# Attention loop regrouped into periods of two head pairs, in an attention and expert-layer kernel

## The chip, the cores and the metric

The kernel runs on one core of a Trainium2 chip. The metric is device time in microseconds (us) for one whole execution: attention over all heads, the routing of tokens to experts, and the expert layers. Five engines work side by side, each through its own queue of instructions in the order of the program: TensorE (PE, with its weight loads PEld), VectorE (DVE), ScalarE (ACT), GpSimd (POOL) and SyncE (SP). An instruction that waits for another engine holds up everything behind it in its own queue.

## The reference: what is computed

```python
def _attn_ref(q, k, v):                      # 8 batches, 12 heads, 448 positions, 64 per head
    scores = scale * np.matmul(q, k.transpose(0, 1, 3, 2)) - np.log(S)
    attn = 1.0 / (1.0 + np.exp(-scores))     # sigmoid, no softmax
    return np.matmul(attn, v)
def _moe_ref(x, w_gate, w1, w2):             # x: the attention's output, 3584 x 768
    # greedy assignment of each token to one of 8 experts by its logit, 448 tokens an expert
    # out[tokens of e] = np.maximum(x[tokens of e] @ w1[e], 0) @ w2[e]
```

Only the attention is touched by the change. Its output feeds the gate's logits, so it is computed almost to single precision.

## The kernel before: how the attention is ordered

The program takes two heads at a time (a **pair**); six pairs make a batch, 48 pairs make the attention. Two pairs, an even and an odd one, share their loads. Here S(p) stands for the scores of pair p, e and o for the even and the odd pair, and a prime for the next two pairs.

**Preparing a pair** (`turn`, lines 484 to 499). DVE transposes the loaded k and q in 32x32 blocks, 128x896 numbers, into the tile `kqT` (line 489). The function returns a second step, `split`: ACT rounds `kqT` to the form `kqH` that TensorE multiplies in one pass (line 497), and DVE takes what the rounding left, `kqL` = `kqT` - `kqH` (line 498). One instruction makes `kqL` for k and q together.

**Scores** (`scores`, line 506). For each of three blocks of 128 keys, six matmuls (line 514): `kqH` by `kqH`, `kqH` by `kqL`, `kqL` by `kqH`, each for both heads. So the second product of a pair's first block already needs the whole of `kqL`. The result goes to a PSUM tile `sc` (three buffers), and ACT's sigmoid (line 504) turns it into `at`. The last 64 keys of both pairs are done together in `rest_scores` (line 524, straight from `kqT`), with a sigmoid of their own.

**Products with v** (`av`, line 529). Six matmuls in full precision (line 538, 12 passes in the trace) add up the three key blocks of a pair in a PSUM tile `tp` (two buffers). For an odd pair, four more (line 544, 8 passes) take the last 64 keys: those of the odd pair into the same `tp`, those of the even pair into a second one. DVE copies the sums into `xt` (line 546) and adds the even pair's remainder (line 548).

**Behind an odd pair.** `turn_rows` (line 601) transposes two pairs of `xt` on DVE into `xz`, which SP stores; after the sixth pair `logits` (line 559) multiplies `xt` by the gate on PE, and DVE adds it up (line 561). These steps wait in a list `bg` and are taken from it one for each pair. `consts` and `scale` are small steps that prepare the routing.

**The order** is written out by hand in the loop of lines 613 to 648, one turn for a pair, a pair's products with v one turn behind its scores. For two pairs the PE does S(e), products of the odd pair before, their last keys, last scores, S(o), products of e. DVE's queue has in each turn: transpose the next pair, `kqL` of the next pair (behind the first scores of the current pair), the copies of the pair before, one step of `bg`.

The loads of k go through SP's queue, those of q through POOL's, into `nkq` (four buffers); DVE's transposes free those buffers. The v tiles `nv` and `nr` have three buffers, freed by the products.

Of the kernel before, what the change touches and what calls it, by code (L numbers as in the profile page):

```python
# [7 lines left out]
F32 = mybir.dt.float32  # L8
# [6 lines left out]
OP = mybir.AluOpType  # L15
# [7 lines left out]
LATE = 1  # L23
# [396 lines left out]
def moe_attention(tc, q, k, v, w_gate, w1, w2, out):  # L420
    nc = tc.nc
    B, H, S, D = q.shape
    DM = H * D
    E, _, F = w1.shape
    CP, NCH, NP, ND, NF = 112, S // 112, H // 2, DM // 128, F // 128
    G4 = 4
    PSUM = bass.MemoryType.PSUM
    with contextlib.ExitStack() as ctx:
# [6 lines left out]
        ps_t = pctx.enter_context(tc.tile_pool(name="pa_t", bufs=2, space=PSUM))  # L435
# [14 lines left out]
        nat = {}  # L450
        LO, HI = slice(0, 64), slice(64, 128)
        def load(b, g, qq=(nc.gpsimd, nc.gpsimd), vq=nc.sync):


            nat["v", b, g] = ld.tile([128, G4, 3, D], F32, name="nv", bufs=3)
            nat["r", b, g] = ld.tile([128, 2, D], F32, name="nr", bufs=3)
            for i in range(2):
                t = nat["kq", b, 2 * g + i] = ld.tile([128, 2, S // 32, 32], F32, name="nkq", bufs=4)
                for n, (qn, src) in enumerate(((nc.sync, k), (qq[i], q))):
                    for j in range(2):  # L460
                        rws = src[b, g * G4 + 2 * i + j].rearrange("(c p) (x d) -> x p c d", p=32, x=2)
                        for x in range(2):
                            o = 64 * j + 32 * x
                            qn.dma_start(t[o:o + 32, n], rws[x])  # L464
            vs = v[b, g * G4:(g + 1) * G4]
            for h in range(G4):
                vq.dma_start(nat["v", b, g][:, h], vs[h, :384].rearrange("(c p) d -> p c d", p=128))
            for i in range(2):
                vq.dma_start(nat["r", b, g][HI if i == 0 else LO],
                             vs[2 * i:2 * i + 2, 384:].rearrange("h p d -> p h d"))  # L470
# [13 lines left out]
        def turn(b, pr, cuts=((0, 2),)):  # L484


            T = KT[b, pr] = wk.tile([128, 2, S], F32, name="kqT", bufs=3)
            for x, y in cuts:
                nc.vector.transpose(T[:, x:y].rearrange("p n t -> p (n t)"),  # L489
                                    nat["kq", b, pr][:, x:y].rearrange("p n c d -> p (n c d)"))  # L490
            H = wk.tile([128, 2, S], F32R, name="kqH")
            L = wk.tile([128, 2, S], F32R, name="kqL")
            KQ[b, pr] = [x[:, i] for i in range(2) for x in (H, L)]

            def split():
                for x, y in cuts:
                    nc.scalar.activation(H[:, x:y], T[:, x:y], AF.Copy)  # L497
                    nc.vector.tensor_tensor(L[:, x:y], T[:, x:y], H[:, x:y].bitcast(F32), OP.subtract)  # L498
            return split

        AT = {}
# [4 lines left out]
        def scores(b, pr, c):  # L506


            a = AT[b, pr, c] = wk.tile([128, 2, S], F32, name="at", bufs=AT_BUFS)
            p = ps_s.tile([128, 2, 512], F32, name="sc")  # L510
            KH, KL, QH, QL = KQ[b, pr]
            for i, (R, M) in enumerate(((KH, QH), (KH, QL), (KL, QH))):
                for j, half in enumerate((LO, HI)):
                    nc.tensor.matmul(p[:, j, :S], R[half, c * 128:(c + 1) * 128], M[half], start=i == 0, stop=i == 2)  # L514
            sigmoid(a, p)

        def rest_scores(b, pr):


            a = AT[b, pr, 3] = wk.tile([128, 2, S], F32, name="at", bufs=AT_BUFS)  # L520
            p = ps_s.tile([128, 2, 512], F32, name="sc")
            for o, T in ((HI, KT[b, pr - 1]), (LO, KT[b, pr])):
                for j, half in enumerate((LO, HI)):
                    nc.tensor.matmul(p[o, j, :S], T[half, 0, S - 64:S], T[half, 1], start=True, stop=True)
            sigmoid(a, p)

        XT = {}

        def av(b, pr, end=False):


            if pr == 0:
                XT[b] = xa.tile([128, NP, S], F32, name="xt", bufs=XT_BUFS)
            p = ps_t.tile([128, 512], F32, name="tp")
            g, h0 = (2 * pr) // G4, (2 * pr) % G4
            for c in range(3):
                for j in range(2):
                    nc.tensor.matmul(p[j * 64:j * 64 + 64, :S], nat["v", b, g][:, h0 + j, c, :],  # L538
                                     AT[b, pr, c][:, j, :], start=(c == 0), stop=(c == 2 and pr % 2 == 0))
            if pr % 2:  # L540
                r = ps_t.tile([128, 512], F32, name="tp")
                for j in range(2):
                    for half, o in ((HI, r), (LO, p)):
                        nc.tensor.matmul(o[j * 64:j * 64 + 64, :S], nat["r", b, g][half, j, :],
                                         AT[b, pr, 3][half, j, :], start=o is r, stop=True)
            (nc.scalar.copy if end else nc.vector.tensor_copy)(XT[b][:, pr, :], p[:, :S])
            if pr % 2:
                nc.vector.tensor_tensor(XT[b][:, pr - 1, :], r[:, :S], XT[b][:, pr - 1, :], OP.add)

        LE = rw.tile([128, 2, CP], F32, name="LE", bufs=1)  # L550
        nc.gpsimd.memset(LE, 0.0)
# [1 line left out]
        def logits(b, prs):  # L553

            s, g = b % 4, b // 4
            p = ps_t.tile([128, 512], F32, name="tp")
            for pr in prs:
                for c in range(NCH):
                    nc.tensor.matmul(p[32 * c:32 * c + 32, :CP], wgz[:, pr, s, :], XT[b][:, pr, c * CP:(c + 1) * CP],
                                     start=(pr == prs[0]), stop=(pr == prs[-1]))  # L560
            nc.vector.tensor_tensor(LE[:, g], LE[:, g], p[:, :CP], OP.add)
# [35 lines left out]
        def turn_rows(b, pr):  # L597

            if pr == 1:
                XR[b] = xa.tile([128, S // 32, NP, 32], F32, name="xz", bufs=XZ_BUFS)  # L600
            nc.vector.transpose(XR[b].rearrange("p i r j -> p r i j")[:, pr - 1:pr + 1],
                                XT[b][:, pr - 1:pr + 1].rearrange("p r (i t) -> p r i t", t=32))
            if pr == NP - 1:
                for a in range(4):
                    nc.sync.dma_start(xs[b * S:(b + 1) * S, 192 * a:192 * a + 192].rearrange("(i t) c -> t i c", t=32),
                                      XR[b][32 * a:32 * a + 32].rearrange("t i r j -> t i (r j)"))

        pairs = [(b, pr) for b in range(B) for pr in range(NP)]
        NPR = len(pairs)
        turn(*pairs[0], ((0, 1), (1, 2)))()  # L610
        bg, late = [], []
        consts = route_consts(nc, cp, K)
        for i in range(NPR + 1):
            cur = pairs[i] if i < NPR else None
            nxt = pairs[i + 1] if i + 1 < NPR else None
            old = pairs[i - 1] if i else None
            if cur and cur[1] % 2 == 0:
                nx = i // 2 + 2
                if nx < NPR // 2:
                    load(nx // 3, nx % 3)  # L620
            split = turn(*nxt) if nxt else None
            for c in range(3 if cur else 0):
                scores(*cur, c)
                if c == 0 and split:
                    split()
            if bg and not cur:
                bg.pop(0)()
            if old:
                av(*old, not cur)
            if cur and cur[1] % 2 == 0:  # L630
                rest_scores(*nxt)
            if i > 2:
                next(consts, None)
            if bg and cur:
                bg.pop(0)()
            if old == (B - 1, NP - 2):
                bg.append(lambda: logits(B - 1, range(NP - 2)))
            if old and old[1] % 2 and old[0] < B - LATE:
                bg.append(lambda b=old[0], pr=old[1]: turn_rows(b, pr))
            if old and old[1] == NP - 1:  # L640
                b = old[0]
                if b < B - 1:
                    bg.append(lambda b=b: logits(b, range(NP)))
                if b in (3, 4):
                    scaled = scale() if b == 3 else scaled
                    bg.append(lambda: next(scaled))
                for c in range(NCH if b >= B - LATE else 0):
                    late.append(lambda b=b, c=c: late_rows(b, c))
        for f in bg:
            f()  # L650
        logits(B - 1, [NP - 2, NP - 1])

        pctx.close()
# [372 lines left out]
```

## Time and profile before

| | us |
|---|---|
| median of three runs | 846.31 (845.62 to 850.72) |
| the profiled execution, its time | 850.65 |
| its span, first to last instruction | 848.9 |
| attention, first `rest_scores` to the last one's start | 11.15 to 264.52 |
| PE busy, share of the span | 94% |
| DVE, ACT, POOL busy | 59%, 48%, 55% |

The trace gives, for each instruction, its start and duration, and the idle time before it with what ended that time. A matmul's end is modelled, and matmuls overlap: what a pass costs is the distance between two starts, not its duration. For short runs of equal instructions the timeline merges neighbours and gives their count. In this document "pitch" is the distance between the starts of two neighbours on one engine.

The span has three parts: the attention, to about 275 us; the choice of the first expert's tokens, with PE mostly idle, to about 300 us; then eight expert layers.

### The profile page before, as it was taken

To read this page: it belongs to the slowest core of one execution; us is meant where nothing else is said; L and a number is where in the kernel's file an instruction comes from. 1 tells how busy PE (TensorE), PEld (TensorE's weight loads), DVE (VectorE), ACT (ScalarE), POOL (GpSimd) and SP (SyncE) were. 2 spreads that over 40 slices of the span, in tenths; PEclk is the share of its full clock that TensorE was granted. 3 is DMA by queue.
4 is the path that set the end of the run, shared out by engine and by line. 5 is a ranking of instruction groups with operands and counts; after the bars stand their busy time and mean duration, and the time that the engine had idled before them with its cause. 6 is when DMAs were issued, how large, how long until landed. Compare 5 with 4: busy or idle time off the path is not lost. (4 is left out here: it accounts for less than half of the span.)

```text
span 848.9 us, 14982 instructions
## 1 busy us (share of the span) xinstructions
PE 800.0 (94%) x5150; PEld 616.0 (73%) x5150; DVE 502.6 (59%) x1426; ACT 409.7 (48%) x506; POOL 467.1 (55%) x446
## 2 busy tenths in 40 slices
PE   6999999999999259899999999999999998999996
PEld 3454544554544149889989999989889887889996
DVE  4677666667663768568568558568678563232150
ACT  6777777777775143333433433433433423541421
POOL 9744444444420035745865875874874883481661
PEclk9999999999999669999999999999999999999998
DMA  8887877777770262365566576575665664845733
GB/s 171 169 179 155 185 172 159 167 177 154 176 151 19 94 186 70 100 183 164 176 196 189 146 207 197 156 211 162 187 199 169 169 210 126 241 138 138 226 130 131
DMA packets 259705, 138.71 MB, mean 163 GB/s; under 512 B 187136, under 2 KB 248832, under 8 KB 259616
## 3 DMA queue, kind: packets, MB, share of 16 engines
q1 hardware_dynamic: 246880, 104.14, 48.1%
q0 software_dynamic: 10880, 33.28, 13.0%
q8 instruction: 41, 0.67, 0.3%
q10 hardware_dynamic: 1856, 0.23, 0.2%
q14 instruction: 48, 0.39, 0.2%
HBM read 105.02 MB, written 32.57 MB: 162 GB/s over the span
## 5 line engine op out<-in xcount | busy, mean ns | idle before, releaser
L716 POOL TENSOR_TENSOR wl<-wr,wh 128x768 fp32r<-128x768 f32 (+1 forms) x96 | 203.5, 2133 | 68.9 <-ACT wh L714 66.0
L504 ACT ACTIVATE at<-sc,bias 128x896 f32<-128x896 f32 x168 | 161.6, 1004 | 40.7 <-PE sc L514 23.3
L464 POOL DMA_DIRECT2D nkq<-in_q_dram x188 | 118.5, 643 | 113.3 <-DVE kqT L489 106.1
L895 PE MATMUL sc<-hh,wh 128*128 128x448 f32 (+2 forms) x400 | 148.5, 371 | 0.4 <-ACT yt L827 0.4
L897 PE MATMUL sc<-hl,wh 128*128 128x448 f32 (+2 forms) x400 | 146.6, 367 | 0.0
L899 PE MATMUL sc<-hh,wl 128*128 128x448 f32 (+2 forms) x400 | 146.6, 366 | 0.0
L714 ACT ACTIVATE wh<-wr 128x768 fp32r<-128x768 f32 (+1 forms) x112 | 101.7, 937 | 92.1 <-PE sc L897 67.6
L862 PE MATMUL sc<-xh,wl 128*128 128x448 f32 (+2 forms) x396 | 144.8, 366 | 0.0
L858 PE MATMUL sc<-xh,wh 128*128 128x448 f32 (+2 forms) x396 | 144.1, 364 | 0.2 <-ACT xh L765 0.2
L860 PE MATMUL sc<-xl,wh 128*128 128x448 f32 (+2 forms) x396 | 144.2, 364 | 0.0
L870 POOL TENSOR_TENSOR hl<-yt,hh 128x896 fp32r<-128x896 f32 x32 | 68.1, 2129 | 96.0 <-ACT yt L869 84.8
L538 PE MATMUL tp<-at,nv 128*64 128x448 f32 x576 | 118.8, 548 | 0.0
L866 ACT ACTIVATE hh<-sc 128x896 fp32r<-128x896 f32 x32 | 29.5, 921 | 142.1 <-PE sc L862 142.1
L498 DVE TENSOR_TENSOR kqL<-kqT,kqH 128x896 fp32r<-128x896 f32 (+1 forms) x49 | 52.5, 1073 | 56.6 <-ACT kqH L497 56.5
L895 PEld LDWEIGHTS sc<-hh,wh 128*128 128x128 f32 x400 | 78.3, 196 | 4.6 <-ACT yt L827 0.6
L897 PEld LDWEIGHTS sc<-hl,wh 128*128 128x128 f32 x400 | 78.3, 196 | 4.6 <-issue 0.9
L899 PEld LDWEIGHTS sc<-hh,wl 128*128 128x128 f32 x400 | 78.3, 196 | 3.8 <-issue 0.2
L860 PEld LDWEIGHTS sc<-xl,wh 128*128 128x128 f32 x396 | 75.6, 191 | 6.0 <-DVE xl L766 0.4
L538 PEld LDWEIGHTS tp<-at,nv 128*64 128x64 f32 x576 | 37.1, 136 | 59.1 <-issue 56.7
L858 PEld LDWEIGHTS sc<-xh,wh 128*128 128x128 f32 x396 | 75.7, 191 | 5.8 <-ACT xh L765 0.4
L862 PEld LDWEIGHTS sc<-xh,wl 128*128 128x128 f32 x396 | 75.6, 191 | 5.7
L736 POOL DMA_INDIRECT xr<-xs,r_idx x32 | 32.0, 1001 | 72.8 <-ACT wh L714 57.2
(187 smaller groups left out, 1115.7 us busy)
## 6 DMA issues: line engine op xcount, KB each, us to landing
wr<-in_moe_w_dram SPq DMA_DIRECT2D x64, 384.0 KB
wr<-in_moe_w_dram SPq DMA_DIRECT2D x48, 512.0 KB
nkq<-in_k_dram SPq DMA_DIRECT2D x192, 56.0 KB
nkq<-in_q_dram POOLq DMA_DIRECT2D x188, 56.0 KB, 2.9
ys<-yt SPq DMA_DIRECT2D x92, 112.0 KB
xs<-xz SPq DMA_DIRECT2D x28, 336.0 KB
nv<-in_v_dram SPq DMA_DIRECT2D x92, 96.0 KB
xr<-ys SPq DMA_DIRECT2D x21, 384.0 KB
```

The lines of the kernel that those rows point to most:

```text
L464: qn.dma_start(t[o:o + 32, n], rws[x])
L504: nc.scalar.activation(a, p[:, :, :S], AF.Sigmoid, bias=bias, scale=1 / math.sqrt(D))
L538: nc.tensor.matmul(p[j * 64:j * 64 + 64, :S], nat["v", b, g][:, h0 + j, c, :], AT[b, pr, c][:, j, :], start=(c == 0), stop=(c == 2 and pr ...
L714: nc.scalar.activation(hi, raw[u], AF.Copy)
L716: eng.tensor_tensor(lo, raw[u], hi.bitcast(F32), OP.subtract)
L858: nc.tensor.matmul(ph[:, f, lo:hi], wh[:, a, fs], xh[:, dd, lo:hi], start=st, stop=False)
L860: nc.tensor.matmul(ph[:, f, lo:hi], wh[:, a, fs], xl[:, dd, lo:hi], start=False, stop=False)
L862: nc.tensor.matmul(ph[:, f, lo:hi], wl[:, a, fs], xh[:, dd, lo:hi], start=False, stop=en)
L870: nc.gpsimd.tensor_tensor(h2, h0, h1.bitcast(F32), OP.subtract)
L895: nc.tensor.matmul(py[:, d2, :w], wh[:, a, dsl], h1, start=st, stop=False)
L897: nc.tensor.matmul(py[:, d2, :w], wh[:, a, dsl], h2, start=False, stop=False)
L899: nc.tensor.matmul(py[:, d2, :w], wl[:, a, dsl], h1, start=False, stop=(j == 1 and a == 3))
```

## The change

The loop runs over the 24 even pairs; one turn is a **period** of two pairs. `av` is cut in two: `av` does the three key blocks of a pair, and copies the sum for an even pair only; `av_rest` does the last keys of both pairs, the copy of the odd one and the addition. In a period PE does S(e), `av_rest` of the period before, the last scores, S(o), products of e, products of o. The transposes of the next pairs stand behind the last scores (even) and behind the products of e (odd), and both splits of the next period stand between the products of e and those of o, behind one step of `bg`.

```diff
-        def av(b, pr, end=False):
+        AVP = {}
+        def av(b, pr):
             if pr == 0:
                 XT[b] = xa.tile([128, NP, S], F32, name="xt", bufs=XT_BUFS)
-            p = ps_t.tile([128, 512], F32, name="tp")
+            p = AVP[b, pr] = ps_t.tile([128, 512], F32, name="tp")
...
-            if pr % 2:
-                r = ps_t.tile([128, 512], F32, name="tp")
-                for j in range(2):
-                    for half, o in ((HI, r), (LO, p)):
-                        nc.tensor.matmul(o[j * 64:j * 64 + 64, :S], nat["r", b, g][half, j, :],
-                                         AT[b, pr, 3][half, j, :], start=o is r, stop=True)
+            if pr % 2 == 0:
+                nc.vector.tensor_copy(XT[b][:, pr, :], p[:, :S])
+
+        def av_rest(b, pr, end=False):
+            p, g = AVP.pop((b, pr)), (2 * pr) // G4
+            r = ps_t.tile([128, 512], F32, name="tp")
+            for j in range(2):
+                for half, o in ((HI, r), (LO, p)):
+                    nc.tensor.matmul(o[j * 64:j * 64 + 64, :S], nat["r", b, g][half, j, :],
+                                     AT[b, pr, 3][half, j, :], start=o is r, stop=True)
             (nc.scalar.copy if end else nc.vector.tensor_copy)(XT[b][:, pr, :], p[:, :S])
-            if pr % 2:
-                nc.vector.tensor_tensor(XT[b][:, pr - 1, :], r[:, :S], XT[b][:, pr - 1, :], OP.add)
+            nc.vector.tensor_tensor(XT[b][:, pr - 1, :], r[:, :S], XT[b][:, pr - 1, :], OP.add)
...
+        evens = [(b, pr) for b in range(B) for pr in range(0, NP, 2)]
+        turn(*evens[0], ((0, 1), (1, 2)))()
+        split = turn(0, 1)
...
+        def finish(b, pr):
+            if b < B - LATE:
+                bg.append(lambda: turn_rows(b, pr))
+            elif pr == NP - 3:
+                bg.append(lambda: logits(b, range(NP - 2)))
+            if pr == NP - 1:
+                bg.append(lambda: logits(b, range(NP)))
+                if b in (3, 4):
+                    scaled = finish.scaled = scale() if b == 3 else finish.scaled
+                    bg.append(lambda: next(scaled))
+        def spare():
+            if bg:
+                bg.pop(0)()
+        for i, (b, pr) in enumerate(evens):
+            if i + 2 < len(evens):
+                load((i + 2) // 3, (i + 2) % 3)
+            nxt = evens[i + 1] if i + 1 < len(evens) else None
+            for c in range(3):
+                scores(b, pr, c)
+                if i == 0 and c == 0:
+                    split()
+            if i:
+                av_rest(evens[i - 1][0], evens[i - 1][1] + 1)
+                finish(evens[i - 1][0], evens[i - 1][1] + 1)
+            rest_scores(b, pr + 1)
+            splits = [turn(*nxt)] if nxt else []
+            for c in range(3):
+                scores(b, pr + 1, c)
+            if i > 1:
+                next(consts, None)
+            av(b, pr)
+            if nxt:
+                splits.append(turn(nxt[0], nxt[1] + 1))
+            spare()
+            for f in splits:
+                f()
+            if i > 1:
+                next(consts, None)
+            av(b, pr + 1)
+            if i + 1 < len(evens):
+                spare()
+        while bg:
+            spare()
+        av_rest(B - 1, NP - 1, True)
```

The replaced loop is lines 608 to 650 of the listing above. In the changed file `turn_rows` transposes on line 606, `av` copies on line 542 and `av_rest` copies and adds on lines 552 and 553; the products are on line 539, the last keys on line 550, and the logits' addition is on line 566.

What this does to DVE's queue, in the third batch (batch 2). Before, from the copy of pair 0's products on: `kqT_1291` and `kqT_1345` are transposes of the next two pairs, `kqL_1294` and `kqL_1348` their splits.

```order
L546 COPY xt_1102<-tp_1255 128x448
L601 STREAM_TRANSPOSE xz_1263<-xt_1102 128x2x14x32
L489 STREAM_TRANSPOSE kqT_1291<-nkq_1000 128x896
L498 TENSOR_TENSOR kqL_1294<-kqT_1291,kqH_1293 128x896
L546 COPY xt_1102<-tp_1324 128x448
L548 TENSOR_TENSOR xt_1102<-tp_1331,xt_1102 128x448
L489 STREAM_TRANSPOSE kqT_1345<-nkq_1118 128x896
L498 TENSOR_TENSOR kqL_1348<-kqT_1345,kqH_1347 128x896
```

After, from the copy of the odd pair's products on, over one period: `kqT_1345` and `kqL_1348` belong to the next even pair, `kqT_1384` and `kqL_1387` to the next odd pair.

```order
L552 COPY xt_1100<-tp_1271 128x448
L553 TENSOR_TENSOR xt_1100<-tp_1331,xt_1100 128x448
L489 STREAM_TRANSPOSE kqT_1345<-nkq_1157 128x896
L542 COPY xt_1100<-tp_1376 128x448
L489 STREAM_TRANSPOSE kqT_1384<-nkq_1166 128x896
L606 STREAM_TRANSPOSE xz_1265<-xt_1100 128x2x14x32
L498 TENSOR_TENSOR kqL_1348<-kqT_1345,kqH_1347 128x896
L498 TENSOR_TENSOR kqL_1387<-kqT_1384,kqH_1386 128x896
```

The eight instructions of a period are the same. Before, each split stands directly behind its own transpose and ahead of a copy; after, the copy of the even pair's sums, the odd pair's transpose and the step of `turn_rows` stand between the even pair's transpose and its split, and both splits are neighbours.

PE's queue at the place of the products. Before, the odd pair's products stand between the scores of the next even pair and the last keys:

```order
L514 MATMUL sc<-kqH,kqL 128x448 x2
L538 MATMUL tp<-at,nv 64x448 x6
L544 MATMUL tp<-at,nr 64x448 x4
L524 MATMUL sc<-kqT 64x448 x4
L514 MATMUL sc<-kqH 128x448 x2
```

After, the products of both pairs stand together, directly ahead of the next even pair's scores:

```order
L514 MATMUL sc<-kqH,kqL 128x448 x2
L539 MATMUL tp<-at,nv 64x448 x12
L514 MATMUL sc<-kqH 128x448 x2
L514 MATMUL sc<-kqL,kqH 128x448 x2
L514 MATMUL sc<-kqH,kqL 128x448 x2
```

The number of matmuls is unchanged; one of the two places at which products with v stand between scores is gone, and the last keys follow scores instead of products.

On ACT, a period was four sigmoids, a rounding, three sigmoids, a rounding; it is now seven sigmoids and then two roundings.

More of the change, by code (lines that the diff above doesn't have):

```diff
@@ L606, in turn_rows @@
                                       XR[b][32 * a:32 * a + 32].rearrange("t i r j -> t i (r j)"))
-        pairs = [(b, pr) for b in range(B) for pr in range(NP)]
-        NPR = len(pairs)
-        turn(*pairs[0], ((0, 1), (1, 2)))()
+        evens = [(b, pr) for b in range(B) for pr in range(0, NP, 2)]
+        turn(*evens[0], ((0, 1), (1, 2)))()
+        split = turn(0, 1)
         bg, late = [], []
         consts = route_consts(nc, cp, K)
[L613 to L624, printed above, removed]
-                    split()
[L626 to L632, printed above, removed]
-                next(consts, None)
[L634 to L648, printed above, removed]
@@ L649, in moe_attention @@
-        for f in bg:
-            f()
+        def finish(b, pr):
[11 more added lines that the diff above has]
+                bg.pop(0)()
@@ L651, in moe_attention @@
+        while bg:
+            spare()
+        av_rest(B - 1, NP - 1, True)
+        for c in range(NCH):
+            late.append(lambda c=c: late_rows(B - 1, c))
         logits(B - 1, [NP - 2, NP - 1])
```

## The prediction

> **What bounds the kernel now.** I read the table by stretches of time first, then one period in the timeline, then the groups by line. Where the attention runs evenly, PE has no free time:
>
> ```profile
> core 0: us, PE busy (x) PEld busy (x) DVE busy (x) ACT busy (x) POOL busy (x), PEclk, DMA share, GB/s
> 99.76:110.34 10.58, 10.58 (x80) 5.20 (x76) 6.99 (x10) 8.30 (x9) 5.03 (x8) 1.00 0.80 158
> ```
>
> In this period of 10.58 us PE is busy for 10.58 at full clock, DVE for 6.99, ACT for 8.30. PE sets the time; DVE has a third of it free. Whether that third can be used depends on when it comes, so here is the next period in the timeline (start, duration, engine; behind it the idle time before and its releaser):
>
> ```profile
> 99.69 0.61 DVE L548 TENSOR_TENSOR xt<-tp,xt 128x448 f32<-128x448 f32 x1
> ...
> 104.25 0.47 PE L514 MATMUL sc<-kqH 64*128 64x448 f32 x2
> 104.37 0.62 DVE L546 COPY xt<-tp 128x448 f32<-128x448 f32 x1 [0.53 <-PE tp L538]
> 104.56 0.36 PE L514 MATMUL sc<-kqL,kqH 64*128 64x448 f32 x2
> 104.91 1.10 DVE L601 STREAM_TRANSPOSE xz<-xt 128x896 f32<-128x896 f32 x1
> ...
> 105.17 1.01 ACT L504 ACTIVATE at<-sc,bias 128x896 f32<-128x896 f32 x1 [0.65 <-PE sc L514]
> ...
> 105.94 1.07 DVE L489 STREAM_TRANSPOSE kqT<-nkq 128x896 f32<-128x896 f32 x1
> 105.98 0.37 PE L514 MATMUL sc<-kqH,kqL 64*128 64x448 f32 x2
> 106.27 2.48 PE L538 MATMUL tp<-at,nv 128*64 128x448 f32 x12
> 107.10 0.95 ACT L497 ACTIVATE kqH<-kqT 128x896 fp32r<-128x896 f32 x1 [0.92 <-DVE kqT L489]
> ...
> 108.08 1.09 DVE L498 TENSOR_TENSOR kqL<-kqT,kqH 128x896 fp32r<-128x896 f32 x1 [1.08 <-ACT kqH L497]
> 108.68 0.98 PE L544 MATMUL tp<-at,nr 64*64 64x448 f32 x8
> 109.48 0.93 PE L524 MATMUL sc<-kqT 64*64 64x448 f32 x8
> 109.73 0.62 DVE L546 COPY xt<-tp 128x448 f32<-128x448 f32 x1 [0.55 <-PE tp L544]
> 110.27 0.61 DVE L548 TENSOR_TENSOR xt<-tp,xt 128x448 f32<-128x448 f32 x1
> 110.34 0.47 PE L514 MATMUL sc<-kqH 64*128 64x448 f32 x2
> 110.56 1.91 ACT L504 ACTIVATE at<-sc,bias 128x896 f32<-128x896 f32 x2 [0.72 <-PE sc L524]
> ...
> 112.44 2.48 PE L538 MATMUL tp<-at,nv 128*64 128x448 f32 x12
> ...
> 114.85 0.47 PE L514 MATMUL sc<-kqH 64*128 64x448 f32 x2
> ```
>
> PE's blocks, start to start: scores 2.02, products 2.41 (106.27 to 108.68), last keys 0.80, last scores 0.86, scores 2.10, products 2.41, together 10.60. On DVE the split at 108.08 ends at 109.17, 1.17 us before the scores that need it start at 110.34. That is the margin of one half period, and DVE was idle for 1.08 just before it. So before, each split has room; the question is how much room the new order leaves.
>
> **The change, part by part.** PE first. The matmuls are the same, so are the two blocks of scores. Products follow products once instead of scores following them. The expense of a switch is visible on leaving scores: 105.98 to 106.27 is 0.29, an ordinary step between pairs of passes is 0.20 (104.56 and 105.98 are seven steps apart, 1.42). Products to last keys shows none (12 passes in 2.41). After the change, the scores are still left twice a period, once for the last keys. So I take 0; the bound is one switch of 0.09 less in 24 periods, -2.2 us, and on the other side nothing beyond the waits below.
>
> DVE next. A is the moment at which PE has finished the even pair's products and starts those of the odd pair. From A on DVE does: copy, transpose of the next odd pair, `turn_rows`, split of the next even pair. None of them can be done earlier, since the copy waits for A and stands first.
>
> - The copy starts 0.12 after PE's next block (104.25, 104.37), and the next instruction 0.54 later (104.91).
> - Each of the two transposes has the size of the one at 104.91, whose successor starts 1.03 later (105.94). The pitch of line 489's transpose to a ready successor isn't shown; its rows (mean below) say 1.09 against 1.10, so I take 1.03 for both and 1.09 as the upper end.
> - The split lasts 1.09 (108.08). PE's second product of the scores reads it. How soon PE follows is seen once, at the start:
>
> ```profile
> 6.69 1.16 DVE L498 TENSOR_TENSOR kqL<-kqT,kqH 128x448 fp32r<-128x448 f32 x2
> 7.23 0.74 PE L514 MATMUL sc<-kqH 64*128 64x448 f32 x2 [7.23 <-ACT kqH L497]
> 7.90 0.74 PE L514 MATMUL sc<-kqL,kqH 64*128 64x448 f32 x2
> 8.81 0.58 PE L514 MATMUL sc<-kqH 64*128 64x448 f32 x2
> 9.19 0.58 PE L514 MATMUL sc<-kqL,kqH 64*128 64x448 f32 x2
> ```
>
> The split ends at 7.85 and PE goes on at 7.90: 0.05. Sum: 0.12 + 0.54 + 1.03 + 1.03 + 1.09 + 0.05 = **3.86 us after A**. PE is there earlier: the odd pair's products take 2.41 and the first product of the scores 0.31 (104.25 to 104.56), so PE wants the split at A + 2.72. **It waits 1.14 us.** Behind the waiting matmul stand the rest of the scores, the last keys and the next products; ACT's sigmoids and DVE's next copy wait with them. The whole period moves, and since the next A moves as well, the DVE chain hangs on it again: nothing is regained. ACT isn't in this chain. In the new period A comes 2.02 + 0.80 + 0.86 + 2.10 + 2.41 = 8.2 us after the start; the first sigmoid starts 0.92 after the scores (104.25, 105.17), seven at 0.96 (110.56, two in 1.91) end near 7.7, and the rounding of 0.95 (107.10) at 8.7, A + 0.5, long before DVE reaches the split. The transpose that it rounds follows the copy and addition behind the last keys (109.73, 110.27) and is done near 5.2.
>
> How many periods pay this:
>
> ```profile
> L601 DVE STREAM_TRANSPOSE xz<-xt 128x896 f32<-128x896 f32 x20 | 22.0, 1102 | 0.0
> L489 DVE STREAM_TRANSPOSE kqT<-nkq 128x896 f32<-128x896 f32 x43 | 46.8, 1089 | 1.3 <-DMA xs<-xz 0.5
> 121.00 1.36 PE L559 MATMUL tp<-xt,wgz 128*32 128x112 f32 x48
> 122.29 0.47 PE L514 MATMUL sc<-kqH 64*128 64x448 f32 x2
> ```
>
> Seven batches have three `turn_rows` each, 21 in all (the window of this view, 30 to 275 us, holds 20). In the periods that also have `logits` (one a batch, 7), those matmuls now stand between the odd pair's products and the next scores: 1.29 us (121.00 to 122.29) of cover, so PE wants the split at A + 4.01 and doesn't wait. In two periods a step of `scale` takes the place ahead of the splits and `turn_rows` comes behind them. That leaves **12 periods at 1.14: 13.7 us**. Two periods without `turn_rows` (first, last but one) wait 3.86 - 1.03 - 2.72 = 0.11 each. The `scale` steps:
>
> ```profile
> L568 DVE TENSOR_REDUCE s_m<-s_a 128x1 f32<-128x112 f32 x1 | 0.3, 270 | 0.0
> L566 DVE TENSOR_SCALAR s_a<-LE 128x112 int32<-128x112 int32 x1 | 0.2, 208 | 0.0
> 192.89 0.32 PE L571 MATMUL tp<-ident,s_m 128*128 128x128 f32 x1
> 193.14 0.47 PE L514 MATMUL sc<-kqH 64*128 64x448 f32 x2
> 193.54 0.28 DVE L572 TENSOR_REDUCE s_m<-tp 128x1 f32<-128x128 f32 x1
> 194.75 1.11 DVE L489 STREAM_TRANSPOSE kqT<-nkq 128x896 f32<-128x896 f32 x1
> ```
>
> The first adds 0.48 to 0.11, so 0.6; the second takes 1.21 on DVE (193.54 to 194.75) against 0.25 more on PE, so 1.1. Sum: 13.7 + 0.2 + 0.6 + 1.1 = **15.6 us**.
>
> Loads cost nothing: the odd pair's transpose, which frees `nkq`, moves from the start of a period to A of the one before, some 2.4 us earlier, and SP's and POOL's order of transfers is unchanged. `xs` stores wait for `turn_rows` a little later and hold up the next k loads in SP's queue, which are read only in the period after next; if that cover failed, DVE's transposes would wait, as they do now for 1.3 us in all. The tail behind the last scores holds the same work in the same order, and the expert layers are untouched.
>
> The profiled execution took 850.65 us, 4.3 above the median; its attention would lengthen by 15.6, to 866.2. Set on the median: 846.31 + 15.6 = **862**.
>
> **The rivals.**
>
> *The splits slip past (not slower).* If DVE took a ready instruction ahead of one that waits, the even pair's split could run before A, once ACT has rounded, and PE would find it ready; the time would be 846.3 less at most 2.2: 845. It decides as soon as three long DVE instructions no longer lie between A and A + 2.72. Against it: `turn_rows` at 104.91 reads sums whose last addition ended at 100.30 (the row at 99.69), DVE was idle for 0.53, and yet it started only behind the waiting copy.
> The Trainium skill, in "TensorE: Matmul & The Clock Gate", section "Architectural detail: the array is 16× 32×32, not 1× 128×128", says that ScalarE's and VectorE's queues are strictly first in, first out. By that rule the time would be 862 and not 845, and the row at 104.91 agrees.
>
> *The gaps cool PE (much slower).* At the start, PE's passes come 0.37 or 0.38 apart (8.81 to 9.19) where they later come 0.20 apart, for the 3.9 us from 7.23 until 11.15. If each wait brought that back, 3.9 us would do the work of 2.1 and lose 1.8. With 13 waits near 1.1 us that is 23: 885.
>
> ```profile
> 11.15 0.98 PE L524 MATMUL sc<-kqT 64*64 64x448 f32 x8
> 275.00 0.59 PE L559 MATMUL tp<-xt,wgz 128*32 128x112 f32 x16 [0.82 <-DVE xt L548]
> 275.52 0.87 PE L591 MATMUL sc<-ident,xt 128*112 128x128 f32 x6
> 290.00:300.00 10.00, 2.08 (x37) 1.52 (x37) 6.94 (x22) 1.58 (x2) 0.42 (x1) 0.50 0.24 79
> ```
>
> The clock is 0.50 where PE works for 2.08 of 10 us; here it would work for nine tenths of each period. After the gap of 0.82 at 275 the 16 short products still take only 0.52.
> The same page of the Trainium skill, section "HAM oscillation — how this bites in real kernels", puts the gap that costs the clock at about 3.4 us; by that rule gaps of 1.1 would leave 862 as it is, and the two gaps of the trace agree with it.
>
> *A shorter chain (about even).* If the long DVE instructions overlap more at their ends than the pitch of 1.03 says, or the waiting matmul catches up later in the period, perhaps half of each wait is left: 15.6 / 2 gives 854. Nothing in the rows speaks for it except that the pitch of two kinds is assumed.
>
> **How the numbers follow.** A measurement of this kernel tells about 1% from no change, 8.5 us. The forecast, 862, has a chance of 0.82 and its own range 857 to 866: 12 waits between 1.0 and 1.26 (both transposes at 1.09), with or without the 2.2. The half wait has 0.08, the cooled PE 0.05, the slipped splits 0.05. The range reaches down to the half wait and up to the forecast plus the 4.3 by which one execution lies above the median: 854 to 867. Faster by over 1% has 0.02 and comes from the splits slipping past, whose other 0.03 is within 1%, with 0.05 of the half wait: 0.08. The rest is slower: 0.90.
>
> **What would show it.** Right: a period is about 11.7 us, PE's busy time per period stays 10.6, and a wait of 1.1 us stands before the second product of the even pair's scores, released by DVE's `kqL` of line 498, in 12 periods, not in those with `logits`. DVE then runs four instructions without idle time from the copy of line 542 to the split. Wrong: periods at 10.6 with the split ending before the scores; passes 0.37 apart after a wait; or an idle DVE inside that chain, which would put the cause with ACT's rounding or a load.

## The result, and the profile after

The changed kernel takes 860.96 us (median of four runs, 859.82 to 862.61), the kernel before 846.70 (845.62 to 850.72). The ratio is 1.0161, with a 95% interval of 1.0133 to 1.0190: slower by 1.6%. The forecast was 862.

Two rows of the table by stretches, the changed kernel's: an ordinary period, from the start of one `rest_scores` to the next (line 524), and a period with `logits`.

```profile
core 0: us, PE busy (x) PEld busy (x) DVE busy (x) ACT busy (x) POOL busy (x), PEclk, DMA share, GB/s
92.90:104.65 11.75, 10.70 (x80) 5.29 (x76) 6.79 (x8) 8.29 (x10) 5.03 (x8) 1.00 0.87 205
116.62:128.37 11.75, 11.75 (x129) 6.40 (x124) 6.97 (x9) 8.30 (x11) 5.02 (x8) 1.00 0.56 122
```

The period was 10.58 us with PE busy throughout; it is 11.75 with PE busy for 10.70. The clock is 1.00 in both, DVE and ACT do the same work as before. The period with `logits` is full: PE busy for all of its 11.75, which is a little less than the 11.87 to 11.95 that such a period took before.

The timeline of the changed kernel over the place in question (the row of products at 107.59, and what follows until the next scores run):

```profile
107.59 4.73 PE L539 MATMUL tp<-at,nv 128*64 128x448 f32 x24
...
109.31 0.96 ACT L497 ACTIVATE kqH<-kqT 128x896 fp32r<-128x896 f32 x1
...
110.12 0.62 DVE L542 COPY xt<-tp 128x448 f32<-128x448 f32 x1 [3.04 <-PE tp L539]
...
110.88 1.11 DVE L489 STREAM_TRANSPOSE kqT<-nkq 128x896 f32<-128x896 f32 x1
...
111.91 1.07 DVE L606 STREAM_TRANSPOSE xz<-xt 128x896 f32<-128x896 f32 x1
112.08 0.95 ACT L497 ACTIVATE kqH<-kqT 128x896 fp32r<-128x896 f32 x1 [1.81 <-DVE kqT L489]
112.25 0.47 PE L514 MATMUL sc<-kqH 64*128 64x448 f32 x2
...
112.91 2.05 DVE L498 TENSOR_TENSOR kqL<-kqT,kqH 128x896 fp32r<-128x896 f32 x2
...
114.01 0.47 PE L514 MATMUL sc<-kqL,kqH 64*128 64x448 f32 x2 [1.29 <-DVE kqL L498]
```

DVE waits 3.04 us for the even pair's products and then runs copy, transpose, `turn_rows` and split without a gap. The rounding that the split reads was done at 110.27, 2.64 us before DVE came to it. PE starts the next scores at 112.25, and their second product waits for the split until 114.01, idle for 1.29 (1.05 in the other ordinary periods; this one is 0.22 longer than they are). All of PE's waits in the attention but one are of this kind, by the list of waits (12 to 288 us, PE alone; total, times, longest). The other one is taken up below.

```profile
PE sc L514 <- DVE kqL L498: 13.4, 13, 1.3
PE tp L539 <- ACT kqH L497: 0.5, 1, 0.5
```

What DVE waits for has changed places. The groups by line, before (30 to 275 us; behind the second bar the idle time ahead of the group) and after (30 to 290 us):

```profile
L498 DVE TENSOR_TENSOR kqL<-kqT,kqH 128x896 fp32r<-128x896 f32 x43 | 47.0, 1093 | 50.8 <-ACT kqH L497 50.8
```

```profile
L498 DVE TENSOR_TENSOR kqL<-kqT,kqH 128x896 fp32r<-128x896 f32 x44 | 45.3, 1068 | 0.1
L552 DVE COPY xt<-tp 128x448 f32<-128x448 f32 x22 | 13.7, 625 | 37.5 <-PE tp L550 37.5
L542 DVE COPY xt<-tp 128x448 f32<-128x448 f32 x22 | 13.7, 625 | 66.3 <-PE tp L539 66.3
```

In the kernel before, DVE was idle for 50.8 us ahead of its splits, waiting for ACT; now it is idle for 104 us ahead of the copies, waiting for PE, and has nothing left ahead of the splits. DVE still has free time, even more of it (it is busy for 6.79 of 11.75), but that time lies before the copies, where the work behind them cannot use it.

From the first `rest_scores` to the last one's start the attention takes 268.38 us (11.20 to 279.58) against 253.37: 15.0 more. The profiled executions differ by only 11.8 in span, because the expert layers, the same program in both, took 3.3 us less in this execution (581.1 from 279.58 to the end, against 584.4); the medians differ by 14.3.

### The profile page after: what moved, and what is told of

Read it like the earlier page. It is cut to its first block, busy times and chain, and to the rows that moved or that the text cites. A ratio compares the mean times of both kernels' runs of the same rounds, so it can differ in the third digit from the quotient of the medians.

```text
span 860.7 us, 15010 instructions
## 1 busy us (share of the span) xinstructions
PE 799.9 (93%) x5150; PEld 617.3 (72%) x5150; DVE 497.4 (58%) x1426; ACT 409.0 (48%) x506; POOL 467.4 (54%) x446
## 5 line engine op out<-in xcount | busy, mean ns | idle before, releaser
L504 ACT ACTIVATE at<-sc,bias 128x896 f32<-128x896 f32 x168 | 156.3, 1007 | 42.2 <-PE sc L514 38.0
L539 PE MATMUL tp<-at,nv 128*64 128x448 f32 x576 | 114.0, 544 | 0.5 <-ACT kqH L497 0.5
L539 PEld LDWEIGHTS tp<-at,nv 128*64 128x64 f32 x576 | 39.1, 137 | 62.8 <-issue 51.5
L514 PE MATMUL sc<-kqL,kqH 64*128 64x448 f32 x288 | 55.3, 381 | 13.6 <-DVE kqL L498 13.4
```

Source lines behind the costliest of these rows:

```text
L504: nc.scalar.activation(a, p[:, :, :S], AF.Sigmoid, bias=bias, scale=1 / math.sqrt(D))
```

## The experiments

The first four ran on one chip, where the kernel before takes 849.98 us (median of 23 runs); the last two, one run each, beside a run of 849.65. No time of the changed kernel beside these is on record: where one is needed, 849.98 times its ratio of 1.0161 gives 863.7, an estimate.

**1. `turn_rows` behind the splits.** It stays in the period, but leaves the chain.

```diff
-            spare()
             for f in splits:
                 f()
+            spare()
```

> The changed kernel with one edit: the step taken from the list (turn_rows, scale) stands behind both splits, not ahead of them. Theory (DVE's chain of copy, transpose, turn_rows and split between the even pair's products and the next scores): the chain is one transpose of 1.03 us shorter, 2.8 us after A; PE wants the split at about A + 2.56 (the row of products takes 4.66 us where two apart took 4.82), so a wait of 0.1 to 0.3 us is left of 1.30, periods of 10.6 to 10.7 us in place of 11.75, about 848 us. Rival, ACT's rounding comes late: the waits stay, 861. Rival, the regrouping itself costs PE time (a burst of seven sigmoids, the loads): 861.

Measured: 851.02, ratio to the kernel before 1.0007 (0.9983 to 1.0031). The same ordinary period, in the table by stretches:

```profile
89.20:99.95 10.75, 10.69 (x80) 5.28 (x76) 6.90 (x8) 8.29 (x11) 5.03 (x8) 1.00 0.93 210
```

One DVE instruction, placed behind two others, takes 1.00 us off an ordinary period. Regrouping and rounding are unchanged in this kernel, so neither of them can have been the cause of that 1.00. A short wait is left: PE's second product starts 0.53 after the first, where 0.31 is its step without a wait.

**2. The rounding earlier.** ACT's half of the even pair's split moves ahead; DVE's half stays.

```diff
             for c in range(3):
                 scores(b, pr + 1, c)
+                if c == 0 and splits:
+                    splits[0](lo=False)
...
-            for f in splits:
-                f()
+            for n, f in enumerate(splits):
+                f(hi=n > 0)
```

> The changed kernel with one edit: ACT's rounding of the next even pair stands behind the first scores of the odd pair, some 2 us earlier; DVE's split stays where it is. Theory (DVE's chain): no change, 861 us, since the split waits for DVE's own queue and not for the rounding. Rival, the rounding behind seven sigmoids is late: the waits of 1.3 us go, 847 us or less.

Measured: 864.03, ratio 1.0163 (1.0119 to 1.0207), the same as the changed kernel's 1.0161. The timeline of this kernel, whose lines from the split on are numbered two higher:

```profile
107.19 0.95 ACT L498 ACTIVATE kqH<-kqT 128x896 fp32r<-128x896 f32 x1
...
112.56 2.05 DVE L500 TENSOR_TENSOR kqL<-kqT,kqH 128x896 fp32r<-128x896 f32 x2
113.67 0.47 PE L516 MATMUL sc<-kqL,kqH 64*128 64x448 f32 x2 [1.29 <-DVE kqL L500]
```

The split was free to run at 108.14 and ran at 112.56, and PE waited 1.29 as before. The rounding is out, and a ready DVE instruction did not pass the waiting copy.

**3. `turn_rows` twice.** Its transpose is issued a second time, with the same operands.

```diff
-            nc.vector.transpose(XR[b]...[:, pr - 1:pr + 1], XT[b][:, pr - 1:pr + 1]...)
+            for _ in range(2):
+                nc.vector.transpose(XR[b]...[:, pr - 1:pr + 1], XT[b][:, pr - 1:pr + 1]...)
```

> The changed kernel with turn_rows' transpose done twice, so DVE gets 21 more instructions of 1.03 us; each period has more than 4 us of DVE left over. Theory (DVE's chain): 12 periods wait 1.03 us longer, and the 7 periods with logits, whose cover just suffices (chain 3.8 us, PE wants the split at about 3.85), begin to wait 1.0 us; 19 x 1.03 = 19.6, about 880 us. Rivals (rounding, regrouping): DVE has free time, 861 us.

Measured: 893.54 (two runs), ratio 1.0506 (1.0450 to 1.0563). That is about 30 us above the estimate for the changed kernel, not 20. Three neighbouring periods, the first with `logits`:

```profile
91.28:104.16 12.88, 11.97 (x128) 6.40 (x124) 8.76 (x20) 7.76 (x10) 5.01 (x8) 1.00 0.33 84
104.16:118.56 14.40, 12.19 (x80) 6.36 (x76) 7.90 (x9) 9.06 (x11) 5.01 (x8) 0.88 0.79 170
118.56:131.45 12.89, 10.69 (x80) 5.28 (x76) 7.90 (x9) 7.75 (x10) 5.02 (x8) 1.00 0.79 157
```

The third period is the expected one: 12.89, 1.14 more than 11.75. The first shows the cover of `logits` used up: it was full at 11.75 and now has 0.91 without PE work. The second is 1.5 us longer than the third, with more PE time for the same 80 matmuls and a granted clock of 0.88. Its timeline behind the wait:

```profile
114.45 0.74 PE L514 MATMUL sc<-kqL,kqH 64*128 64x448 f32 x2 [2.21 <-DVE kqL L498]
114.99 0.58 PE L514 MATMUL sc<-kqH,kqL 64*128 64x448 f32 x2
115.36 0.58 PE L514 MATMUL sc<-kqH 64*128 64x448 f32 x2
115.73 0.58 PE L514 MATMUL sc<-kqL,kqH 64*128 64x448 f32 x2
```

The passes come 0.37 apart, as in the first microseconds of the program. Seven of the 12 periods are of this sort. So the cooled PE of the rival, which the changed kernel doesn't show, appears in most of these periods when the gap is 2.2 us. Nineteen waits of 1.15 more and seven times 1.5 give 32, against 32.7 in the attention of this trace.

**4. The even pair's split ahead of the copy.** Rounding and split stand together behind the first scores of the odd pair.

```diff
             for c in range(3):
                 scores(b, pr + 1, c)
+                if c == 0 and splits:
+                    splits.pop()()
```

> The changed kernel with one edit: rounding and split of the next even pair stand together behind the first scores of the odd pair, so that DVE does the split in the idle time ahead of its copy. Theory (DVE's chain): no wait is left, periods are PE's own 10.43 us (10.58 less the 0.16 that the row of products saves), 23 x 0.16 = 3.6 us under the kernel before: 843 us. Rival, the regrouping itself costs PE time: above 847 us, up to 861.

Measured: 845.74 (12 runs), ratio 0.9954 (0.9930 to 0.9977): faster than the kernel before by 0.5%, and, by the two ratios, than the changed kernel by about 2%. In the table by stretches and the timeline of this kernel:

```profile
88.02:98.44 10.42, 10.42 (x81) 5.28 (x77) 7.00 (x8) 8.30 (x10) 5.02 (x8) 1.00 0.87 205
```

```profile
102.29 1.09 DVE L498 TENSOR_TENSOR kqL<-kqT,kqH 128x896 fp32r<-128x896 f32 x1 [1.43 <-ACT kqH L497]
...
103.90 0.62 DVE L542 COPY xt<-tp 128x448 f32<-128x448 f32 x1 [0.52 <-PE tp L539]
...
106.04 0.47 PE L514 MATMUL sc<-kqH 64*128 64x448 f32 x2
106.35 0.36 PE L514 MATMUL sc<-kqL,kqH 64*128 64x448 f32 x2
106.54 0.36 PE L514 MATMUL sc<-kqH,kqL 64*128 64x448 f32 x2
```

PE is busy for all of 10.42, and the second product follows the first after its ordinary 0.31. The order of matmuls is that of the changed kernel. So the regrouping by itself is worth 0.16 us in an ordinary period, and the place of one DVE instruction cost 1.33. Over the whole attention of the two traces it is worth 2.3 us (251.05 against 253.37); the rest of the 4.2 between the medians is not explained.

**5 and 6. Gaps of other lengths.** After experiment 3 the question was at which gap the clock falls. Half of the transpose more, and the whole of it three times:

```diff
# 5
+            nc.vector.transpose(XR[b]...[:, pr - 1:pr], XT[b][:, pr - 1:pr]...)
# 6, in the loop of experiment 3
+            for _ in range(3):
```

> The changed kernel with half of turn_rows' transpose done a second time (one pair, 128x448): some 0.55 us more in DVE's chain, 21 times. Theory (DVE's chain): PE's idle gap before the second product grows from 1.30 to about 1.85 us, 12 periods of 12.3 us, and about 0.5 in the periods with logits; 19 x 0.55 = 10.5 us, about 872 on a chip where the kernel before takes 847. Second question, the clock: with gaps of 2.2 us, 7 of 12 periods came out at 14.4 us in place of 12.9, with passes 0.37 apart. If the gap has to outlast some window near 2 us, no period here is 1.5 us longer; if the share of cold periods grows evenly with the gap, a few of 12 are.

> The changed kernel with turn_rows' transpose done three times: 2.1 us more in DVE's chain. Theory (DVE's chain): gaps of about 3.4 us in 12 periods, 13.95 us each where the clock stays up, and 2.2 us in the 7 with logits; 19 x 2.15 = 41, about 902 us where the kernel before takes 847. The clock: if every gap of 3.4 us brings PE down, the 12 periods are 15.5 us and some of the 7 are 1.5 longer too, 920 to 930 us.

Measured: 888.66 and 936.36 (one run each, beside 849.65). Periods of both by the table by stretches, experiment 5 first, each with its clock:

```profile
22.53:34.94 12.41, 10.68 (x80) 5.28 (x76) 7.42 (x9) 8.28 (x10) 9.49 (x18) 1.00 0.81 175
34.94:48.94 14.00, 12.26 (x82) 6.21 (x77) 7.43 (x9) 9.42 (x11) 6.86 (x19) 0.88 0.75 143
```

```profile
116.34:132.58 16.24, 12.90 (x80) 6.52 (x76) 9.00 (x10) 9.41 (x10) 5.02 (x8) 0.82 0.77 161
223.10:237.14 14.04, 10.69 (x80) 5.28 (x76) 10.47 (x12) 8.28 (x10) 5.03 (x8) 1.00 0.77 151
```

Where the clock stays up, the periods are 12.41 and 14.04, 0.66 and 2.29 above the changed kernel's: with 1.14 for one more transpose, the chain goes into the period in full. But the guess that a window near 2 us protects shorter gaps was wrong, and experiment 6 came out above the 920 to 930 us foreseen for it. The idle time ahead of the second product and the number of the 12 periods whose clock falls below 1.00 are:

| kernel | idle, us | periods below 1.00, of 12 |
|---|---|---|
| changed kernel | 1.05 (once 1.29) | 0 |
| half more | 1.73 | 7 |
| twice | 2.20 | 7 |
| three times | 3.35 | 11 |

The length of the gap does not decide alone. In experiment 6 the seven periods with `logits` have gaps of 2.06 us, once 2.30. From the end of the gap to the end of the period the clock is 1.00 in six of them and lower in one (here the first and the fifth):

```profile
66.00:68.61 2.61, 2.61 (x24) 1.78 (x28) 1.46 (x4) 1.90 (x3) 0.00 (x0) 1.00 0.89 206
248.56:252.40 3.84, 3.84 (x24) 2.18 (x28) 1.12 (x2) 2.81 (x3) 0.00 (x0) 0.65 0.89 213
```

On PE, these periods differ from the others by the 48 short matmuls of `logits` ahead of the gap; whether they are the reason was not tried.

## Why the prediction was right

**DVE's chain after A: right, with two small errors that cancel.** In the trace A itself has no row, since the 24 passes are one row, but the copy starts 2.53 after the products do, as before (2.41 + 0.12). From the copy on, the sum had 3.74 to PE's product; the ordinary period has 11.75 where 10.60 + 1.14 = 11.74 was foreseen. In the period before the one shown that stretch took 3.66 (98.37 to 102.03), 0.08 less than the sum. Against it, PE's next step behind the wait takes 0.31 (102.03 to 102.34), where 0.20 is ordinary. In the period shown above the odd pair's transpose started 0.76 instead of 0.54 after the copy; that period is the only one of 11.97 (experiments 1, 2 and 4 have a step of 0.74 to 0.77 in the same place), and what held the transpose up is open.

**The count: right, but for one period right by luck.** Thirteen waits of PE for the split are in the list: 11 of 1.05 or 1.06 us, the one of 1.29, and one of 0.49 in the first period with `scale`; those with `logits` show none. The second `scale` period is 11.72 where 10.59 + 1.1 was foreseen, but not for the reason given. Before the split PE is idle there for only 0.05; its wait of 0.52, the other one in the list, stands between the two pairs' products:

```profile
203.78 0.62 DVE L542 COPY xt<-tp 128x448 f32<-128x448 f32 x1 [3.05 <-PE tp L539]
...
204.51 2.48 PE L539 MATMUL tp<-at,nv 128*64 128x448 f32 x12 [0.52 <-ACT kqH L497]
```

The rounding that the row names had ended at 203.93; the copy ended at 204.40. The step's own matmul takes a `tp` tile between the two pairs' products, there are two such tiles, and the copy frees the one that the odd pair needs. This reading fits the order in the program and the times, but no run tried it. Experiment 4, which has no wait for the split left, has the same 0.52 and still takes 11.44 for this period. So most of this term was not DVE's chain.

**The switch between kinds of matmul: wrong by its size and its bound.** The step took 0 for it, with 0.09 a period as the most. The row of 24 passes takes 4.66 (107.59 to 112.25) where two rows of 12 took 4.82, 0.16 less. The two rows of 12 had looked like passes 0.20 apart without a switch; within the row of 24, weight loads come in pairs 0.375 apart, so 0.1875 a pass, and each row's rest is its switch. In the changed kernel this did not shorten the period, because the end of the chain is fixed by the even pair's products and not by the odd pair's: PE came 0.16 earlier and waited 0.16 longer. Experiment 4 shows it as time, 10.42 a period.

**The sum.** Foreseen 15.6 for the attention, measured 15.0. The sum counted the two `scale` steps in full and forgot what they cost in the kernel before (its two intervals of 10.68 and the one of 12.15, about 0.4 together), and the periods with `logits` are 0.1 to 0.2 shorter each. Against that, the 12 waiting periods cost 14.2 and not 13.7. On the medians, 14.3. So part of the closeness of the total is luck.

**The rivals.** The slipped splits are refuted by experiment 2: a split ready for 4.4 us stayed behind the copy. It agrees with the rule of the Trainium skill that the prediction cites ("TensorE: Matmul & The Clock Gate", section "Architectural detail: the array is 16× 32×32, not 1× 128×128"), that VectorE's queue is strictly first in, first out. The half wait did not occur. The cooled PE did not occur at 1.05 us of idle time, and its mechanism was real: at 1.73 us and more, most ordinary periods of experiments 3, 5 and 6 show it. The rule of the Trainium skill cited with it (the same page, section "HAM oscillation — how this bites in real kernels"), that a gap must last about 3.4 us, agrees with the changed kernel, and not with the gaps of 1.73 and 2.20; the measurement decides. So this part of the forecast was right by less margin than its text thought: the gaps of 1.05, and the one of 1.29, lie 0.7 and 0.4 us below those of 1.73.

## What to carry to other kernels

An engine with free time can still end up on the critical path if its free time lies before an instruction that waits and its work behind it: add up the chain from the wait to the consumer, not the load over the period. Before work is regrouped on the bounding engine, look at what the other engines' queues hold between their wait and the next thing it needs, and put that thing ahead of the wait. If a change loses, one instruction's place may be all of it: here the regrouping was worth 0.5% by the medians, 0.3% by the attention of the traces, and one split behind a copy turned that into 1.6% the other way.

## What the hardware showed beyond that

PE's clock can fall after short idle gaps: 1.73 us of idle time in a period of 12.4 cost a lower clock in 7 of 12 periods; 1.05 in a period of 11.75 did so in none of 11. A fallen clock shows as passes 0.37 apart in place of 0.20 and made a period 1.1 to 2.8 us longer (13.55 against 12.41 in experiment 5, 16.8 against 14.04 in experiment 6, where the longest also begin at the low clock that the gap before them left). The loss then grows faster than the wait that causes it (experiment 3: 20 us expected, 30 measured). In these ordinary periods it begins somewhere between 1.05 and 1.73 us; a gap of 1.29 was seen once in the changed kernel and once in experiment 2, at full clock, too few to narrow this down. No single length is the rule: behind `logits`, gaps of 2.06 to 2.30 left the clock at 1.00 six times out of seven. What else it depends on was not tried.
